# Routing tokens to experts with the 24 best of 16 groups, slots by counting, and matmuls on zeros

## The chip, the cores and the metric

The kernel runs on one core of a Trainium2 chip. The metric is the device time of one execution in microseconds (us). The engines of the core work side by side, each through its own queue in order: TensorE (PE in the profile; its weight loads are PEld), VectorE (DVE), ScalarE (ACT), GpSimd (POOL), and the DMA queues, most of them filled by SyncE (SP). SBUF is the working memory of 128 partitions; PSUM is the memory that TensorE writes.

## The reference

Attention over 8 batches, 8 heads, 576 positions and 64 dimensions, in which each query keeps its 32 best keys. The heads side by side give 4608 tokens of 512 features, and each token goes to one of 8 experts; each expert takes only its 80 tokens of highest gate weight.

```python
scores = scale * np.matmul(q, k.transpose(0, 1, 3, 2))
kth = np.partition(scores, -top_k, axis=-1)[..., -top_k:-top_k + 1]
scores = np.where(scores >= kth, scores, -1e9)
attn = softmax(scores); x = (attn @ v) as (4608, 512)
logits = x @ w_gate                         # (4608, 8)
expert_idx = np.argmax(logits, axis=1)
gate_w = probs[np.arange(N), expert_idx]    # softmax of the logits
for e in range(E):
    tok_idx = where(expert_idx == e)
    if len(tok_idx) > capacity:             # capacity is 80
        keep = np.argpartition(-gate_w[tok_idx], capacity)[:capacity]
        tok_idx = tok_idx[keep]
    h = np.maximum(x[tok_idx] @ w1[e], 0.0) # 512 -> 1024
    out[tok_idx] = gate_w[tok_idx, None] * (h @ w2[e])
```

All other rows of the output are zero.

## The kernel before, in words

**Attention** (`Attention.run`) goes over 32 pairs of heads, each in 5 blocks of queries (four of 128, one of 64 in which the two heads share the partitions). One block of 128 queries of one head is a unit; there are 288. The order of work of all engines is written out by hand, in `step`, as a pipeline over units: VectorE searches the threshold of a unit (`parts`, `search`), GpSimd makes the mask (`below`, L239), TensorE forms scores, turns them and multiplies with v, ScalarE copies and exponentiates. The end of each pair of heads writes its token features to HBM and adds to the logits (`norm`). Every second batch, after its last pair of heads, `gates` turns the logits of the two batches into gate weights: VectorE finds the maximum, a one-hot of the first best expert (`oh`, L359 to L362) and the gate weight (`gw`, L365 to L367). GpSimd multiplies the one-hot with the token number and with the gate weight and writes both to `R` (L376): 128 partitions, two kinds, 40 token columns, 8 experts. So `gates` runs four times, the last time when attention is done.

`judge` (L466 to L478) makes a flag, `bad`, from the smallest threshold and the smallest sum. It is read at the end of the kernel (L699): if set, a slow exact version of everything runs after.

**Routing** is the first half of `finish` (L511 to L603). One expert's 80 best among 4608 tokens are found in two stages. First, four transposes on TensorE (L534) put the gate weights of `R` on 80 partitions (10 groups by 8 experts), with 512 tokens each, and `best` (L526, L528) finds each partition's 80 best: MAX8 gives eight values, MATCH_REPLACE8 wipes them out, ten times. Then 10 matmuls with slices of the identity (L542) bring the 10 lists of each expert side by side, 800 values on 8 partitions, and `best` finds the 80 best of those. The 80th is the expert's bar. The bar goes to all partitions (L550 to L556); `sel` (L562) marks the tokens above or on it; matmuls with ones and a scan (L569 to L579) number the marked tokens, so that each has a slot from 1 to 80 (L581). `hot` (L588) is the one-hot of the slot, 80 wide, and 40 matmuls (L591) with it as weights gather token numbers and gate weights into `acc`, 80 slots by 16. A matmul of float32 operands is two instructions on TensorE. Four small operations (L594 to L603) make indices of it.

**Experts**: `gather` (L616) fetches the 80 rows of one expert by an indirect DMA, `turn_g` (L626) transposes them, `hidden` (L639) and `product` (L651) multiply, `store` (L660 to L663) transposes back, scales and writes by an indirect DMA. The order is again by hand (L667 to L686). Weights of experts 0 to 3 are loaded during attention; those of expert 4 when attention has ended, and those of experts 5 to 7 when the product of an earlier expert gives its buffer free.

Of the kernel before, what the change touches and what calls it, by code (L numbers as in the profile page):

```python
# [9 lines left out]
F32 = mybir.dt.float32  # L10
BF16 = mybir.dt.bfloat16
I32 = mybir.dt.int32
AX = mybir.AxisListType.X
Act = mybir.ActivationFunctionType
Alu = mybir.AluOpType
PSUM = bass.MemoryType.PSUM
# [4 lines left out]
FAR = 1e-30  # L21
# [4 lines left out]
def kernel(  # L26
# [11 lines left out]
    nc = tc.nc  # L38
# [17 lines left out]
    FK = F // P  # L56
    NG = 6
    G0 = 24
    UPP = 2 * NF + 1
    NU = NP * UPP  # L60

# [9 lines left out]
    nc.gpsimd.memset(zero, 0.0)  # L71
    wg = const.tile([P, HP, E], F32, name="wg")

    R = const.tile([P, 2, NM, E], F32, name="R")
    nc.gpsimd.memset(R, 0.0)
    bad = const.tile([1, 1], I32, name="bad")

# [41 lines left out]
    class Attention:  # L119
# [226 lines left out]
        def gates(self, b0, nb):  # L346

            GM = nb * NK
            lg = self.lg.rearrange("p b c e -> p (b c) e")
            small = lambda sh, name: self.small.tile(sh, F32, name=name, tag=name, bufs=1)  # L350
            mx = small([P, GM], "mx")
            nc.vector.tensor_reduce(mx, lg, axis=AX, op=Alu.max)
            nc.vector.tensor_tensor(out=lg, in0=lg, in1=mx.unsqueeze(2).to_broadcast([P, GM, E]), op=Alu.subtract)
            el = small([P, GM, E], "el")
            yield 0
            nc.scalar.activation(el, lg, Act.Exp)

            oh = small([P, GM, E], "oh")
            nc.vector.scalar_tensor_tensor(out=oh, in0=lg, scalar=0.0, in1=rank.unsqueeze(1).to_broadcast([P, GM, E]),  # L359
                                           op0=Alu.is_ge, op1=Alu.mult)  # L360
            nc.vector.tensor_reduce(mx, oh, axis=AX, op=Alu.max)
            nc.vector.tensor_tensor(out=oh, in0=oh, in1=mx.unsqueeze(2).to_broadcast([P, GM, E]), op=Alu.is_equal)  # L362
            yield 0
            gw = small([P, GM], "gw")
            nc.vector.tensor_reduce(gw, el, axis=AX, op=Alu.add)  # L365
            nc.vector.tensor_scalar(gw, gw, EPS, None, op0=Alu.add)
            nc.vector.reciprocal(gw, gw)  # L367
            yield 0
            ms = bass.ds(b0 * NK, GM)
            for p, cs in ((P, slice(0, NF)), (TL, slice(NF, NK))):  # L370
                sh = [p, nb, cs.stop - cs.start, E]
                o4 = oh.rearrange("p (b c) e -> p b c e", b=nb)[:p, :, cs, :]
                for kind, src in ((0, tok[:, ms]), (1, gw)):
                    r4 = R[:p, kind, ms, :].rearrange("p (b c) e -> p b c e", b=nb)[:, :, cs, :]
                    s4 = src.rearrange("p (b c) -> p b c", b=nb)[:p, :, cs].unsqueeze(3).to_broadcast(sh)
                    nc.gpsimd.tensor_tensor(out=r4, in0=o4, in1=s4, op=Alu.mult)  # L376

        def run(self, slow):

# [83 lines left out]
                    i += 1  # L463
            assert not slow and not due

        def judge(self):  # L466

            small = self.small
            least = small.tile([P, 2], F32, name="least", bufs=1)
            nc.vector.tensor_reduce(least[:, 0:1], thr_all, axis=AX, op=Alu.min)  # L470
            nc.vector.tensor_reduce(least[:, 1:2], z_all.rearrange("p n c h -> p (n c h)"), axis=AX, op=Alu.min)
            nc.vector.tensor_scalar(least[:, 1:2], least[:, 1:2], -FAR, None, op0=Alu.add)
            nc.vector.tensor_tensor(out=least[:, 0:1], in0=least[:, 0:1], in1=least[:, 1:2], op=Alu.min)
            ps = self.ps_c.tile([P, 512], F32, name="tp", tag="cc")
            nc.tensor.transpose(ps[:1, :P], least[:, 0:1], ident)
            low = small.tile([1, 1], F32, name="low", bufs=1)
            nc.vector.tensor_reduce(low, ps[:1, :P], axis=AX, op=Alu.min)
            nc.vector.tensor_scalar(bad, low, 0.0, None, op0=Alu.is_le)  # L478

        def batch(self, b):  # L480

            for hp in range(HP):
# [12 lines left out]
                for _ in self.norm(hp, b, hp, 0, 1):  # L495
                    pass

    def finish(wpool):

        stack = ctx.enter_context(ExitStack())  # L500
        late = stack.enter_context(tc.tile_pool(name="late", bufs=1))
        for dma in load_w(4, late):
            dma()
        sl = stack.enter_context(tc.tile_pool(name="sl", bufs=1))
        routing = stack.enter_context(ExitStack())
        ps_a = routing.enter_context(tc.tile_pool(name="ps_a", bufs=2, space=PSUM))
        ps_b = routing.enter_context(tc.tile_pool(name="ps_b", bufs=4, space=PSUM))

        rt = routing.enter_context(tc.tile_pool(name="rt", bufs=1))
        iot_i = rt.tile([P, cap], I32, name="iot_i")  # L510
        nc.gpsimd.iota(iot_i, pattern=[[1, cap]], base=1, channel_multiplier=0)  # L511
        iot = rt.tile([P, cap], F32, name="iot")
# [4 lines left out]
        before = rt.tile([P, P], BF16, name="before")  # L517
        nc.gpsimd.affine_select(out=before, in_=onesb, compare_op=Alu.is_gt, fill=0.0, base=0,
                                pattern=[[1, P]], channel_multiplier=-1)
        EH = E // 2  # L520
        seg = rt.tile([P, EH, 2 * NM], F32, name="seg")
        nc.gpsimd.memset(seg, 1.0)
        nc.gpsimd.memset(seg[:, :, 0:1], 0.0)
        def best(dst, src):
            for r in range(0, cap, 8):
                nc.vector.max(out=dst[:, r : r + 8], in_=src)  # L526
                if r + 8 < cap:
                    nc.vector.match_replace(out=src, in_to_replace=dst[:, r : r + 8], in_values=src, imm_value=0.0)  # L528


        NH = 10
        cd_ps = ps_b.tile([P, 512], F32, name="cd_ps", tag="b")
        for i in range(NM // NH):
            nc.tensor.transpose(cd_ps[: NH * E, i * P : (i + 1) * P], R[:, 1, i * NH : (i + 1) * NH, :].rearrange("p m e -> p (m e)"), ident)  # L534
        cd = rt.tile([NH * E, NM // NH * P], F32, name="cd")
        nc.vector.tensor_copy(cd, cd_ps[: NH * E, : NM // NH * P])
        top1 = rt.tile([NH * E, cap], F32, name="top1")
        best(top1, cd)
        mg_ps = ps_a.tile([P, 2, 512], F32, name="mg_ps", tag="a")
        GH = NH // 2  # L540
        for g in range(NH):
            nc.tensor.matmul(mg_ps[:E, g // GH, g % GH * cap : (g % GH + 1) * cap], lhsT=ident[: NH * E, g * E : (g + 1) * E],  # L542
# [7 lines left out]
        nc.vector.tensor_scalar_max(thr, top2[:, cap - 1 : cap], 1e-6)  # L550
        thrw = rt.tile([E, P], F32, name="thrw")
        nc.vector.tensor_copy(thrw, thr.to_broadcast([E, P]))
        tb_ps = ps_b.tile([P, 512], F32, name="tb_ps", tag="b")
        nc.tensor.transpose(tb_ps[:, :E], thrw, ident[:E, :E])
        tb = rt.tile([P, E], F32, name="tb")
        nc.vector.tensor_copy(tb, tb_ps[:, :E])  # L556
# [2 lines left out]
        sel = rt.tile([P, E, 2, NM], BF16, name="sel")  # L559
        tbb = tb.unsqueeze(2).to_broadcast([P, E, NM])  # L560
        for i, op in enumerate((Alu.is_gt, Alu.is_equal)):
            nc.vector.tensor_tensor(out=sel[:, :, i, :], in0=R[:, 1, :, :].rearrange("p m e -> p e m"), in1=tbb, op=op)  # L562
        w = rt.tile([P, E, 2, NM], F32, name="w_slot")
        tot = ps_a.tile([P, 2, 512], F32, name="tot", tag="a")
        pos = ps_a.tile([P, 2, 512], F32, name="pos", tag="a")
        C = EH * 2 * NM
        for i in range(2):
            sv = sel[:, i * EH : (i + 1) * EH, :, :].rearrange("p e k m -> p (e k m)")
# [12 lines left out]
        nc.vector.tensor_reduce(slot, w.rearrange("p e k m -> p m (e k)"), axis=AX, op=Alu.add)  # L581


        acc = ps_b.tile([P, 512], F32, name="acc", tag="b")
        CH = NM // 4
        for m0 in range(0, NM, CH):
            hot = rt.tile([P, CH, cap], F32, name="hot", tag="hot", bufs=2)
            nc.vector.tensor_tensor(out=hot, in0=slot[:, m0 : m0 + CH].unsqueeze(2).to_broadcast([P, CH, cap]),  # L588
                                    in1=iot.unsqueeze(1).to_broadcast([P, CH, cap]), op=Alu.is_equal)
            for m in range(m0, m0 + CH):  # L590
                nc.tensor.matmul(acc[:cap, : 2 * E].rearrange("p (k e) -> p k e", k=2), lhsT=hot[:, m - m0, :], rhs=R[:, :, m, :],  # L591
                                 start=(m == 0), stop=(m == NM - 1))
        a2 = sl.tile([cap, 2, E], F32, name="a2")
        nc.vector.tensor_copy(a2, acc[:cap, : 2 * E].rearrange("p (k e) -> p k e", k=2))  # L594
        i1 = a2[:, 0, :]
# [60 lines left out]
        def store(e):  # L656
            ps = ps_x.tile([P, 512], F32, name="yx", tag="x")
            yT = y_t.pop(e)
            for d in range(HP):
# [4 lines left out]
                out=out[:, :], out_offset=bass.IndirectOffsetOnAxis(ap=idx_s[:, e : e + 1], axis=0),  # L664
                in_=y[:, :], element_offset=0, bounds_check=N - 1, oob_is_err=False, in_offset=None)

        with tc.manual_schedule():  # L667
            for e in range(3):
                gather(e)
            turn_g(0)  # L670
            turn_g(1)
            for e in range(E + 1):
                if e < E:
                    hidden(e)
                if e >= 2:
                    store(e - 2)
                if e >= 1:
                    product(e - 1)
                    if 5 <= e + 4 < E:
                        for dma in load_w(e + 4, wpool):  # L680
                            dma()
                if e + 3 < E:
                    gather(e + 3)
                if e + 2 < E:
                    turn_g(e + 2)
            store(E - 1)  # L686
# [3 lines left out]
    with ExitStack() as main:  # L690
# [3 lines left out]
        with ExitStack() as stack:  # L694
            att = Attention(stack, False)
            att.run(slow)
            att.judge()
        finish(wpool)
    with tc.If(nc.values_load(bad[0:1, 0:1]) > 0):  # L699
        for dma in clear():  # L700
            dma()
# [4 lines left out]
        with ExitStack() as again:  # L706
            wpool = again.enter_context(tc.tile_pool(name="wpool2", bufs=4))
            for e in range(4):
                for dma in load_w(e, wpool):
                    dma()  # L710
            finish(wpool)


# [29 lines left out]
```

## Time and profile before

| | before |
|---|---|
| time, median of 3 | 1154.14 us (1153.25 to 1154.17) |
| span of the profiled execution | 1156.5 us |
| TensorE busy | 921.9 us (80%) |
| VectorE busy | 999.5 us (86%) |
| ScalarE busy | 714.0 us (62%) |
| GpSimd busy | 520.7 us (45%) |
| mean granted TensorE clock | 0.922 |

The page of the profile gives busy times of each engine over the span and then, as rows of 40 digits, in equal slices of it: a digit is the busy share in tenths. The row PEclk is the clock that TensorE was granted, in tenths of full speed. The timeline lists work in order of time, and behind it, in brackets, for what the engine waited. In the list of groups, one line has all instructions of one kind from one source line: their count, busy time and mean in ns, then the idle time just before them and what ended it. Windows give busy times of all engines in a chosen stretch.

### The profile page before, as it was taken

How to read it: one execution, taken by the hardware profiler on the slowest of the kernel's cores; microseconds unless marked ns; L12 is line 12 of the kernel's file. 1: busy time of each engine (PE TensorE's matmuls, PEld its weight loads, DVE VectorE, ACT ScalarE, POOL GpSimd, SP SyncE). 2: the span in 40 equal slices, each digit the busy share in tenths (PEclk: the TensorE clock that was granted, in tenths of full speed). 3: DMA queues.
4: the chain of work that ended last, by engine and by line, in shares of the span. 5: the costliest groups of instructions: out<-in, count | busy, mean ns of one | idle time of the engine just before them, and what ended most of it. 6: DMA issues, size and time to landing. Idle time of an engine off the chain costs nothing.

```text
span 1156.5 us, 35811 instructions
## 1 busy us (share of the span) xinstructions
PE 921.9 (80%) x13262; PEld 753.3 (65%) x13262; DVE 999.5 (86%) x5218; ACT 714.0 (62%) x1534; POOL 520.7 (45%) x344
## 2 busy tenths in 40 slices
PE   6988888888888888888888888888888887207897
PEld 3766766666666666676667676666666666207886
DVE  6999999999999999999899999998999998691011
ACT  4777776777677777767677777776777766100110
POOL 2555554555555545555455545545555455001101
PEclk9999998999999899988999989998999988656999
DMA  4144442323232332332132211111111100402830
GB/s 107 34 115 116 115 116 70 79 79 79 79 79 79 79 79 79 79 79 79 48 81 71 62 33 43 39 42 34 42 43 43 43 12 12 156 0 71 312 128 27
DMA packets 167895, 85.77 MB, mean 74 GB/s; under 512 B 117792, under 2 KB 154656, under 8 KB 167712
## 3 DMA queue, kind: packets, MB, share of 16 engines
q1 hardware_dynamic: 166688, 80.78, 25.4%
q0 software_dynamic: 1024, 2.62, 0.7%
q8 instruction: 106, 1.74, 0.6%
q14 instruction: 77, 0.63, 0.2%
HBM read 63.19 MB, written 20.19 MB: 72 GB/s over the span
## 4 chain that ended last, share of the span: by engine, by line
DVE 49%; PE 26%; issue 12%; ACT 9%; POOL 3%; DMA 0%; SPq 0%; DVEq 0%; POOLq 0%; ACTq 0%
DVE cand L204 17%; PE cc L294 7%; DVE y L226 7%; DVE w L228 6%; DVE cand L223 6%; ACT s L197 4%; DVE top L215 3%; PE yp L651 3%; PE sp L169 3%; ACT wT L280 3%; PE ab L271 3%; POOL mask L239 2%; DVE pick L231 2%; DVE w L215 2%; DVE top L526 1%
## 5 line engine op out<-in xcount | busy, mean ns | idle before, releaser
L239 POOL TENSOR_SCALAR mask<-s,thr_all 128x576 bf16<-128x576 f32 x288 | 496.3, 1723 | 477.7 <-DVE cand L223 453.7
L204 DVE MAX8 cand<-s 128x8 f32<-128x96 f32 x1728 | 395.2, 242 | 8.8 <-ACT s L197 8.8
L220 ACT ACTIVATE sign<-s,w 128x576 bf16<-128x576 f32 x288 | 226.2, 786 | 118.1 <-DVE w L215 114.1
L294 PEld LDWEIGHTS cc<-vb,wT 128*64 128x64 f32 x5760 | 217.5, 149 | 36.9 <-ACT wT L280 20.1
L294 PE MATMUL cc<-vb,wT 128*64 128x65 f32 x5760 | 239.4, 236 | 2.6 <-ACT wT L280 1.1
L226 DVE SCALAR_TENSOR_TENSOR y<-s,w 128x576 f32<-128x576 f32 x288 | 228.8, 794 | 0.2 <-issue 0.2
L228 DVE MAX8 w<-y 128x8 f32<-128x576 f32 x288 | 212.3, 737 | 0.0
L192 PE MATMUL sp<-kT,qT 64*128 64x288 f32 (+1 forms) x1280 | 203.6, 438 | 5.0 <-ACT kT L180 2.5
L271 PE MATMUL ab<-ident,s 128*128 128x128 f32 x1152 | 187.6, 294 | 1.2 <-ACT wT L280 1.2
L197 ACT ACTIVATE s<-sp 128x1152 f32<-128x1152 f32 (+1 forms) x160 | 166.8, 1042 | 16.4 <-PE sp L192 16.2
L271 PEld LDWEIGHTS ab<-ident,s 128*128 128x128 f32 x1152 | 136.5, 149 | 25.8 <-ACT wT L280 14.8
L280 ACT ACTIVATE wT<-ab 128x1024 f32<-128x1024 f32 (+1 forms) x160 | 150.6, 941 | 0.0
L276 PEld LDWEIGHTS <-mask 128*128 128x128 bf16 x1440 | 94.9, 99 | 70.4 <-POOL mask L239 68.1
L192 PEld LDWEIGHTS sp<-kT,qT 64*128 64x128 f32 (+1 forms) x1280 | 106.3, 180 | 43.2 <-ACT s L197 4.1
L278 ACT ACTIVATE wT<-cc 128x256 f32<-128x256 f32 (+1 forms) x160 | 58.8, 368 | 108.8 <-PE cc L276 108.8
L276 PE MATMUL cc<-minus,mask 128*128 128x128 bf16 x288 | 64.4, 223 | 59.2 <-POOL mask L239 59.1
L215 DVE MAX8 top<-cand 128x8 f32<-128x48 f32 x576 | 108.0, 187 | 0.1
L223 DVE MATCH_REPLACE8 cand<-top,cand 128x48 f32<-128x48 f32 x576 | 107.8, 187 | 0.0
L276 PE MATMUL ab<-minus,mask 128*128 128x128 bf16 x1152 | 103.2, 221 | 0.0
L315 ACT ACTIVATE xn<-cc,z_all 128x64 f32<-128x64 f32 (+1 forms) x320 | 82.9, 317 | 1.9 <-DVE z_all L306 1.8
L271 PE MATMUL cc<-ident,s 128*128 128x128 f32 x288 | 81.8, 284 | 0.0
L169 PE MATMUL sp<-ident,xn 128*128 128x128 f32 x128 | 26.4, 341 | 42.5 <-ACT s L197 42.5
(164 smaller groups left out, 861.4 us busy)
## 6 DMA issues: line engine op xcount, KB each, us to landing
w<-in_moe_w_dram SPq DMA_DIRECT2D x32, 512.0 KB, 4.0
w<-in_moe_w_dram SPq DMA_DIRECT2D x8, 2048.0 KB, 13.0
out_dram<-zero SPq DMA_DIRECT2D x9, 1024.0 KB, 5.8
qn<-in_q_dram SPq DMA_DIRECT2D x64, 128.0 KB, 3.8
kn<-in_k_dram SPq DMA_DIRECT2D x64, 128.0 KB, 2.9
vb<-in_v_dram SPq DMA_DIRECT2D x64, 128.0 KB, 2.6
xd<-xn SPq DMA_DIRECT2D x32, 256.0 KB, 2.3
qn<-in_q_dram SPq DMA_DIRECT2D x32, 32.0 KB, 3.4
```

Source lines behind the costliest of these rows:

```text
L192: nc.tensor.matmul(o, lhsT=qT[d, t * P : t * P + m], rhs=kT[d, j * HS : (j + 1) * HS], start=True, stop=True)
L197: nc.scalar.activation(s[:, : g * S].rearrange("p (j c) -> p j c", c=HS), ps[:, : 2 * g, :HS], Act.Copy, scale=TINY)
L204: nc.vector.max(out=cand[:, j, :], in_=s[:, j * S // NG : (j + 1) * S // NG])
L220: nc.scalar.activation(sign, s, Act.Sign, bias=w9[:, 7:8], scale=-1.0, accum_out=cnt)
L223: nc.vector.match_replace(out=cand, in_to_replace=dst, in_values=cand, imm_value=LOW)
L226: nc.vector.scalar_tensor_tensor(out=y, in0=s, scalar=w9[:, 7:8], in1=s, op0=Alu.is_lt, op1=Alu.mult)
L228: nc.vector.max(out=w9[:, 8:], in_=y)
L239: nc.gpsimd.tensor_scalar(self.mask[i], self.s[i], self.thr[:, i : i + 1], None, op0=Alu.is_lt)
L271: nc.tensor.matmul(dst[h][c], lhsT=sc[:, keys[c]], rhs=ident, start=c == 0 or (c == NF and h == 0), stop=False, is_transpose=True, skip_gr ...
L276: nc.tensor.matmul(dst[h][c], lhsT=mk[:, keys[c]], rhs=minus, start=False, stop=True, skip_group_check=True)
L280: nc.scalar.activation(wT[:, : g * NF, :], ab.rearrange("p h c r -> p (h c) r")[:, : g * NF, :], Act.Exp, scale=scale / TINY)
L294: nc.tensor.matmul(cc[r : r + TL, o], lhsT=wT[:, j * NF + c if c < NF else 2 * NF + j, r0 : r0 + TL], rhs=vb[:, c, h, :], start=(c == 0), ...
```

## The change

The routing is written anew, in `route`, and the old one stays as `route_all` for the slow exact version alone.

- **Groups.** `R` now holds gate weights only, in an order that lets two transposes and two small matmuls put them on all 128 partitions: 16 groups by 8 experts, with 288 tokens each. `gates` writes it with three products on VectorE instead of four on GpSimd.
- **24 of each group.** The first search finds only the 24 best of each of the 16 groups (3 MAX8 and 2 MATCH_REPLACE8), and `max_index` gives their positions, from which the token number follows. The second search is over 16 x 24 = 384 values.
- **Slots by counts.** Each group counts how many of its 24 reach the bar; a matmul with a triangle mask gives the number in the groups ahead of it. Since each group's list is in descending order, its r-th value has the slot "number ahead + r". One one-hot of the number ahead (`first`, 104 wide), shifted by r, serves all 24 ranks, so 24 matmuls replace 40.
- **The flag.** 24 are enough if no group gives all 24 to one expert; and the number of slots must be 80. Both go into `judge`, which sets the flag to the full version otherwise.
- **The check moved**: `judge` stands behind `hidden(2)` now, since it needs the counts.
- **Zero products**: `warm` issues bf16 matmuls of zeros, 256 columns each, whose result nobody reads: 72 after the lists have been brought together, and 36 after the slots. They are for the TensorE clock.

```diff
-    R = const.tile([P, 2, NM, E], F32, name="R")
+    R = const.tile([P, NK, B, E], F32, name="R")
+    chunks = ((slice(0, 2), slice(0, 3, 2)), (slice(2, 4), slice(1, 4, 2)), (slice(4, 5), slice(4, 5)))
...
-                    nc.gpsimd.tensor_tensor(out=r4, in0=o4, in1=s4, op=Alu.mult)
+                nc.vector.tensor_tensor(out=r4, in0=o4, in1=s4, op=Alu.mult)
...
+        def warm(n):
+            t = ps.tile([P, 2 * P], F32, name="warm", tag="warm", bufs=1)
+            z = zero.bitcast(BF16)
+            for _ in range(n):
+                nc.tensor.matmul(t, lhsT=z[:, :P], rhs=z, start=True, stop=True)
...
+            for r in range(0, TOP, 8):
+                src = cd_ps[:, :GS] if r == 0 else cd[:, r // 8 - 1, :]
+                nc.vector.max(out=top1[:, r : r + 8], in_=src)
+                if r + 8 < TOP:
+                    nc.vector.match_replace(out=cd[:, r // 8, :], in_to_replace=top1[:, r : r + 8], in_values=src, imm_value=0.0)
...
+            for g in range(GB):
+                nc.tensor.matmul(mg_ps[:E, g * TOP : (g + 1) * TOP], lhsT=ident[:, g * E : (g + 1) * E], rhs=top1,
+                                 start=True, stop=True)
+            warm(WARM1)
+            for r in range(0, TOP, 8):
+                nc.vector.max_index(out=ix[:, r : r + 8], in_max=top1[:, r : r + 8],
+                                    in_values=cd_ps[:, :GS] if r == 0 else cd[:, r // 8 - 1, :])
...
+            nc.tensor.matmul(few[:, 0:1], lhsT=ofe.rearrange("k g e -> k (g e)"), rhs=bar8, start=True, stop=True)
...
+            nc.vector.scalar_tensor_tensor(out=taken, in0=top1, scalar=bar, in1=ones, op0=Alu.is_ge, op1=Alu.mult,
+                                           accum_out=count[:, 0:1])
+            nc.tensor.matmul(few2[:, 0:1], lhsT=ahead, rhs=count[:, 0:1], start=True, stop=True)
+            nc.tensor.matmul(few2[:, 1:2], lhsT=same.rearrange("p g e -> p (g e)"), rhs=count[:, 0:1], start=True, stop=True)
...
+            nc.vector.tensor_scalar(first, col, few2[:, 0:1], None, op0=Alu.is_equal)
+            for r in range(TOP):
+                nc.tensor.matmul(acc[:cap, : 2 * E], lhsT=first[:, TOP - r : TOP - r + cap],
+                                 rhs=give[:, r, :, :].rearrange("p k e -> p (k e)"), start=(r == 0), stop=(r == TOP - 1))
+            warm(WARM2)
...
-            att.judge()
-        finish(wpool)
+        finish(wpool, False)
...
+                if e == 2 and not full:
+                    judge()
```

Further preparations of the new routing are a mask of the expert of each partition (`emask`), two masks made from it for the counts (`same`, `ahead`), the column numbers (`col`), and the first token of each group (`base_i`, `bi`, `base`).

## The prediction

> **What bounds the kernel now.** I read the page's slices first, for where the engines are full.
>
> ```profile
> span 1156.5 us, 35811 instructions
> PE   6988888888888888888888888888888887207897
> DVE  6999999999999999999899999998999998691011
> PEclk9999998999999899988999989998999988656999
> ```
>
> A slice is 28.9 us. For 34 slices VectorE (DVE) is at 9: attention is bound by it, and an operation added there costs nearly its full time. Then come two slices in which TensorE (PE) falls to 2 and 0 while its clock is at half: the routing. The timeline shows its edges.
>
> ```profile
> 991.10 0.22 DVE L367 RECIPROCAL gw<-gw 128x10 f32<-128x10 f32 x1
> ...
> 1007.66 2.83 PE L542 MATMUL mg_ps<-top,ident 80*8 80x80 f32 x20 [15.13 <-DVE top L526]
> ...
> 1032.40 1.36 DVE L562 TENSOR_TENSOR sel<-R,tb 128x320 bf16<-128x320 f32 x2
> ...
> 1041.49 10.85 PE L591 MATMUL acc<-R,hot 128*80 128x16 f32 x80 [6.45 <-DVE hot L588]
> ...
> 1058.98 3.94 PE L639 MATMUL hp__17147<-xt,w 128*64 128x80 f32 x64
> ```
>
> (Start and duration in us, then the work, and in brackets what it waited for.) Routing runs as one chain from the end of L367, 991.32, to the first expert matmul of L639, 1058.98: **67.7 us** in which nothing else is on the path. The groups of DVE in 988 to 1058 us say what fills it:
>
> ```profile
> L526 DVE MAX8 top<-mg 8x8 f32<-8x800 f32 x10 | 9.8, 982 | 0.3
> L528 DVE MATCH_REPLACE8 mg<-top,mg 8x800 f32<-8x800 f32 x9 | 8.7, 963 | 0.0
> L526 DVE MAX8 top<-cd 80x8 f32<-80x512 f32 x10 | 6.9, 691 | 0.3
> L528 DVE MATCH_REPLACE8 cd<-top,cd 80x512 f32<-80x512 f32 x9 | 6.0, 671 | 0.0
> ```
>
> Those searches are about 35 us with their loads and gaps. The other view I need is windows, for the clock:
>
> ```profile
> 990.00:995.00 5.00, 0.44 (x1) 0.14 (x1) 3.51 (x11) 0.00 (x0) 0.94 (x4) 0.55 0.94 376
> 1040.00:1052.00 12.00, 10.51 (x79) 10.52 (x80) 4.28 (x5) 0.00 (x0) 0.00 (x0) 0.50 0.00 1
> 1057.00:1062.00 5.00, 4.51 (x54) 4.13 (x56) 0.98 (x2) 0.00 (x0) 2.40 (x3) 0.50 0.43 126
> 1062.00:1067.00 5.00, 5.00 (x136) 4.82 (x134) 0.49 (x1) 0.88 (x2) 0.00 (x0) 0.99 0.14 28
> ```
>
> The columns are busy time of PE, its weight loads, DVE, ACT, POOL, then the granted clock. PE was busy for 10.5 us in L591 and still held at 0.50, so narrow matmuls (16 columns) do not lift the clock; the expert matmuls lift it about 5 us after they begin.
>
> [...] PE idles from 988.9, the clock falls near 990.5, and the edges seen at 970, 976.8, 990.5 and 1062.1 are whole multiples of 3.4 us apart. [...]
>
> **The change, part by part.** The length law first. MAX8 takes 0.98 us on 800 elements and 0.69 on 512, so 0.29 per 288. A MAX8/load/MATCH_REPLACE8 pair takes 2.10 us on 800 (starts 1011.53 to 1013.63) and 1.51 on 512 (993.29 to 994.80): 2.05 ns per element and 0.46 fixed. Partitions do not matter (8 and 80 lie on one line).
>
> *Gates.* Three DVE products replace four on GpSimd. L341, as small, takes 0.19 us in the full stream. Three earlier calls: 9 x 0.19 = **+1.7** (0.9 if they overlap as L598 and L601 do, starting 0.08 apart); I take 1.5. GpSimd loses its four at nothing: it is 45% busy and mostly waits for DVE. In the last call the products come after L367: 0.5. Five small preparations enter DVE's queue among the gates (emask, bi, three on base) where iot leaves it: +0.5 net, between 0.3 and 1.0. bi waits for GpSimd's base_i, the sixth operation from 988.8, at a spacing of 0.15 done by 989.8, before DVE gets there; behind bi would be the whole gate chain, so a late one shows at once.
>
> *Turning R:* two 128x128 transposes, four narrow instructions, at half clock: 0.44 (the last L534) + 0.25 + 0.2 = 0.9.
>
> *First search:* 3 MAX8 and 2 replacements on 288: two pairs of 1.05, one MAX8 of 0.46: **2.6**, where before it was 15.0 with the copy L536.
>
> *Positions:* three index passes. Lower bound, a replacement of the same length with its load, 0.53[...]. I take 0.58, so 1.75, plus three 24-element operations at 0.18: 2.3. They hide the 16 mg matmuls (32 instructions; L542 took 0.14 each at half clock and 80 columns, with 24 columns 0.05, 1.6 us). The old mg wait of 3.0 and copy of 1.0 vanish.
>
> *Second search:* 384 columns instead of 800: nine pairs of 1.25 and one MAX8 of 0.55: **11.7**, before 19.9.
>
> *First zero products (72).* They stand in PE's queue ahead of the bar's matmul few, for which DVE waits. 128x320 bf16 at half clock came every 0.27 (L569, L570), so 256 columns cost 0.21 at half and 0.107 at full. Begun when mg is through, [...] 24 run slow and 48 fast: 10.3 us. DVE needs 0.6 + 11.7 = 12.3 from the same start. So they cost nothing; the work that hides them is the second search. If all ran slow: 15.4, and few is 2.9 late.
>
> *Bar, counts, give.* Clamp, matmul, copy, count: L550 to L556 took 0.92 for such a round trip; with a two-pass matmul and an accumulator read (0.08 in L231's groups) 1.2. Two products, give on 384 (L577 on 320: 0.48, so 0.55), and first: 1.2, beside the two count matmuls.
>
> *Slots.* 24 matmuls in 48 instructions replace 80. L591's 10.85 us over 80 is 0.136 at half clock: **6.5**; at full clock half, 3.3. All of sel, scan, slot and hot goes.
>
> *Second zero products (36)* stand ahead of the gathered tokens' transposes. L591's end to L639 was 6.64 us, waiting for indices and two gathers. [...] the 36 end after some 6.0; two warm transposes and the copy make it 7.05. Then the first half of expert 0 runs warm: 2.2 instead of 3.9, **-1.65**.
>
> *Check moved* into expert 2: seven DVE operations, about 1.9 us, begin after the fourth xt copy while PE has 4.6 us of L639; one PE transpose stays, 0.15. Taking it out of the end of attention gains nothing: L478 ended at 987.9, and DVE then waited for ACT's part until 988.75.
>
> Sum from 991.3 to the first expert matmul: 0.5 + 0.5 + 0.9 + 2.6 + 2.3 + 11.7 + 1.2 + 1.2 + 6.5 + 7.05 = 34.45 instead of 67.7: -33.2. With +1.5, +0.15 and -1.65: **-33.2, 1121 us**. Expert 4's weights, issued at 988.66, move in the windows up to about 1001 and are not met by gathers at 1016 or later; the loads of experts 5 to 7 hang on the products before them and shift along.
>
> **Rivals.**
> *A, clock lost before the slots* (the sum above, 1121). For it: after the zero products PE idles about 3.5 to 5 us, and 988.9 to 992 shows how soon the clock drops; L591 shows that the slots don't raise it.
> *B, clock stays full.* Slots 3.3, no delay by the 36, transposes as the gathers land: 6.4. The stretch is 30.6: 67.7 - 30.6 + 1.65 - 1.65 = -37.1, **1117**. For it: the 72 may run slower than 0.107 each and end nearer to few; against it: the edges must fall well.
> *C, zero products in the way*: half clock throughout, few 2.9 late, the 36 take 7.7, expert 0 not warmed: 1121 + 2.9 + 2.0 + 1.65 = **1127.5**. For it: 970 to 976.8, where PE was full and the clock stayed at half[...]; against it: 1062.
> *D, slower than before.* If a group gave all 24 or a tie broke the count, the flag would run everything again: at least 288 searches of 4 MAX8 at 0.74, so over 1121 + 850 = **1970**. From the inputs of the reference the fullest group gives 16 and no bar ties: hardly.
>
> **How the numbers follow.** A 0.57, B 0.23, C 0.10, a smaller gain from something unseen (a late preparation, instruction fetch) 0.08, D 0.02. The time is A's. Index passes, preparations and gates are worth about 1.5 either way around A and B; the range 1115.5 to 1125 covers both and leaves out C and D. Faster by over 0.2% (2.3 us) 0.97, within 0.005, slower 0.025.
>
> **What would show it.** DVE's searches: pairs of 1.05 and 1.25 us. PE: no wait of DVE's bar on zero products; acc at 0.134 an instruction (A, C) or 0.067 (B); clock by windows of 3 us from the end of the 72; the first L639 group's 64 instructions in 2.2 us. The attention part longer by 1.5. It would be wrong if acc's start came more than 24 us after L367, if DVE waited for a preparation, or if expert matmuls waited for weights now needed 33 us sooner.

## The result

| | before | after |
|---|---|---|
| time, median of 4 | 1153.7 us (1152.95 to 1154.17) | 1118.24 us (1117.08 to 1120.55) |
| ratio to before | | 0.9696 (0.9679 to 0.9713) |
| span of the profiled execution | 1156.5 us | 1118.8 us |
| mean granted TensorE clock | 0.922 | 0.945 |

The change makes the kernel 35.5 us faster. The slices of the page after:

```profile
span 1118.8 us, 35976 instructions
PE   6888888888788888888888888888788888768997
DVE  5999999999999999999999999999899999962111
PEclk9999989999999989998899999999899989987999
```

The two slices in which TensorE stood at 2 and 0, under a clock of 6 and 5, have gone; what is left of them is a slice with TensorE at 6, and a clock of 8 and 7 in that slice and the next. The timeline of the routing, with start and duration in us, the work, and in brackets what it waited for:

```profile
990.98 0.22 DVE L371 RECIPROCAL gw<-gw 128x10 f32<-128x10 f32 x1
991.39 0.37 DVE L379 TENSOR_TENSOR R<-oh,gw 128x32 f32<-128x32 f32 x3
...
992.89 0.47 DVE L638 MAX8 top<-cd_ps 128x8 f32<-128x288 f32 x1 [1.13 <-PE cd_ps L631]
...
995.44 0.46 DVE L648 FIND_INDEX8 ix<-top,cd_ps 128x8 uint32<-128x288 f32 x1
...
996.90 8.92 PE L623 MATMUL warm<-zero 128*128 128x256 bf16 x72
...
997.44 0.55 DVE L660 MAX8 top<-mg_ps 8x8 f32<-8x384 f32 x1
...
1009.05 0.14 DVE L665 TENSOR_SCALAR bar<-top 8x1 f32<-8x1 f32 x1
...
1009.34 0.55 PE L667 MATMUL few<-bar,ofe 8*128 8x1 f32 x2 [3.52 <-DVE bar L665]
...
1011.96 6.59 PE L692 MATMUL acc<-give,first 128*80 128x16 f32 x48 [0.44 <-DVE first L687]
1018.38 6.16 PE L623 MATMUL warm<-zero 128*128 128x256 bf16 x36
...
1025.47 2.13 PE L754 MATMUL hp__17220<-xt,w 128*64 128x80 f32 x52 [0.37 <-DVE xt L743]
```

From the end of L371 (991.20) to L754 (1025.47) it is 34.3 us, instead of 67.7. The 72 zero products end at 1005.8, and TensorE then waits 3.5 us for the bar: they are in nobody's way. The windows of the same execution show the clock (the first number after the busy times and counts of the five engines):

```profile
999.00:1005.00 6.00, 6.00 (x57) 5.38 (x55) 5.65 (x16) 0.00 (x0) 0.00 (x0) 1.00 0.31 119
1006.00:1009.00 3.00, 0.00 (x0) 0.00 (x0) 2.84 (x7) 0.00 (x0) 0.00 (x0) 1.00 0.00 0
1009.00:1012.00 3.00, 1.58 (x7) 1.47 (x7) 1.75 (x10) 0.00 (x0) 0.00 (x0) 0.50 0.00 0
1012.00:1018.00 6.00, 6.00 (x46) 6.00 (x46) 0.00 (x0) 0.00 (x0) 0.00 (x0) 0.50 0.00 0
```

It is full from 998.8, 1.9 us after the 72 begin, until 3 us after their end, and half from 1009 on, just before the work that could have used it: the slots run 6 us at full occupancy and half clock.

### The profile page after: what moved, and what is told of

Read it like the earlier page. It is cut to its first block, busy times and chain, and to the rows that moved or that the text cites. A ratio compares the mean times of both kernels' runs of the same rounds, so it can differ in the third digit from the quotient of the medians.

```text
span 1118.8 us, 35976 instructions
## 1 busy us (share of the span) xinstructions
PE 926.0 (83%) x13353; PEld 755.2 (68%) x13353; DVE 972.1 (87%) x5213; ACT 714.0 (64%) x1534; POOL 515.7 (46%) x332
## 3 DMA queue, kind: packets, MB, share of 16 engines
q8 instruction: 107, 1.75, 0.6%
## 4 chain that ended last, share of the span: by engine, by line
DVE 47%; PE 28%; issue 11%; ACT 10%; POOL 2%; DMA 1%; SPq 0%; DVEq 0%; POOLq 0%; ACTq 0%
DVE cand L208 17%; DVE y L230 7%; PE cc L298 7%; DVE w L232 6%; DVE cand L227 6%; ACT s L201 5%; DVE top L219 4%; PE sp L173 3%; PE yp L766 3%; PE ab L275 3%; ACT wT L284 3%; DVE pick L235 2%; POOL mask L243 2%; DVE w L219 2%; PE sp L196 1%
## 6 DMA issues: line engine op xcount, KB each, us to landing
w<-in_moe_w_dram SPq DMA_DIRECT2D x8, 2048.0 KB, 12.9
```

## The experiments

In the diffs a minus is the changed kernel. "Stretch" is the routing from the last gate reciprocal to the first expert matmul; "attention" ends with that reciprocal; the "tail" goes from the end of expert 0's first 64 instructions to the end of the span. These three come from one profiled execution each, the times and ratios from several executions each, the ratios against executions of the kernel before on the same chip ("160 first" and "before, again" are single executions).

| kernel | time, us | ratio to before | attention | stretch | expert 0, first 64 | tail |
|---|---|---|---|---|---|---|
| before | 1153.7 | | 991.3 | 67.7 | 3.9 | 93.6 |
| before, again | 1154.5 | | 988.2 | 67.7 | 3.8 | 93.0 |
| after | 1118.2 | 0.9696 (0.9679 to 0.9713) | 991.2 | 34.3 | 3.0 | 90.3 |
| after, again | 1118.0 | 0.9691 (0.9677 to 0.9705) | 991.1 | 34.3 | 2.4 | 90.4 |
| no zero products | 1122.8 | 0.9731 (0.9712 to 0.9750) | 993.8 | 34.0 | 4.5 | 92.8 |
| the 36 alone | 1121.6 | 0.9728 (0.9709 to 0.9747) | 987.9 | 34.9 | 2.4 | 93.6 |
| 104 first | 1117.5 | 0.9689 (0.9663 to 0.9716) | 989.7 | 32.3 | 2.4 | 92.3 |
| 160 first | 1124.2 | | 988.4 | 38.0 | 2.4 | 93.7 |
| gates on GpSimd | 1117.5 | 0.9684 (0.9658 to 0.9709) | 987.0 | 34.6 | 2.4 | 91.7 |
| gates eight times | 1132.7 | 0.9835 (0.9813 to 0.9856) | 1001.1 | 34.3 | 2.4 | 89.9 |
| 32 best of a group | 1127.0 | 0.9776 (0.9754 to 0.9798) | 989.2 | 40.8 | 2.4 | 91.6 |
| strips | 1112.7 | 0.9647 (0.9631 to 0.9664) | 989.5 | 29.6 | 2.4 | 91.5 |
| strips, 104 first | 1113.5 | 0.9657 (0.9644 to 0.9671) | 987.6 | 28.9 | 2.4 | 92.8 |
| strips, gates on GpSimd | 1112.8 | 0.9640 (0.9609 to 0.9671) | 989.7 | 29.5 | 2.4 | 91.0 |

**No zero products at all, and the 36 alone.**

```diff
-    WARM1, WARM2 = 72, 36
+    WARM1, WARM2 = 0, 0        # the second kernel: 0, 36
```

> Both groups of zero products are left out (72 and 36). Reference marks of the changed kernel: slots (acc) 6.59 us, from their end to the first expert matmul 6.92, first 64 instructions of expert 0 some 2.8. Account of the prediction (A): the 72 lie beside the second search and the clock has dropped before the slots anyway, so slots stay at 6.5 to 6.6 and the bar's matmul starts as soon as VectorE is done; without the 36 the first expert matmul comes 6.6 us after the slots instead of 6.9, but the first half of expert 0 runs at half clock, 3.9 us. Net 0.6 to 1.3 us slower than the changed kernel: about 1119.2. Rival 1, zero products do hold the clock for something in the routing: 2 us or more slower, 1120.5 or above. Rival 2, they stand in the way: faster than the changed kernel by 0.5 or more.

> The 72 zero products are left out, the 36 stay. Account A: nothing changes, slots 6.5 to 6.6 us at half clock, expert 0 warm, within 0.5 us of the changed kernel (1118.2). Rival, the 72 do something for the bar's and count matmuls (0.55 us each now): slower by 0.5 to 1.

Within the routing the first account held: slots 6.58 us in both, and the stretch 34.0 and 34.9 us. The time of the kernel without any did not fit it: 1122.8 us, where 1119.2 was expected. That lies where rival 1 put it, but not for rival 1's reason, since nothing in the routing got longer. Without the 36 the first expert matmul came 6.7 us after the slots, and the first half of expert 0 took 4.5 us instead of 2.4. This is the timeline of TensorE without zero products:

```profile
1025.85 0.77 PE L741 MATMUL xp<-ident,xg 80*128 80x80 f32 x4 [4.76 <-DMA xg<-xd,idx_x]
1027.04 0.80 PE L741 MATMUL xp<-ident,xg 80*128 80x80 f32 x4 [0.41 <-DMA xg<-xd,idx_x]
1027.76 4.51 PE L754 MATMUL hp__17112<-xt,w 128*64 128x80 f32 x64
```

So the 36 trade 0.3 to 0.9 us of delay for 2.1 us in expert 0: worth 1.2 to 1.8 us, an estimate from these profiles. The ratios of the two kernels, 0.9731 and 0.9728, have intervals of 0.002 to either side, too wide to show it. With the 36 alone:

```profile
1008.66 6.58 PE L692 MATMUL acc<-give,first 128*80 128x16 f32 x48 [0.44 <-DVE first L687]
1015.08 6.77 PE L623 MATMUL warm<-zero 128*128 128x256 bf16 x36
...
1022.78 2.44 PE L754 MATMUL hp__17148<-xt,w 128*64 128x80 f32 x64 [0.37 <-DVE xt L743]
```

The slots take the same 6.58 us. Its expected time, within 0.5 us of the changed kernel, missed: it is 3.3 us slower by the medians. In the profile the stretch is 0.6 us longer (the 36 took 6.77 us instead of 6.16) and the tail 3.2; that the two profiled executions are nonetheless equally long, 1118.8 us, is due to an attention 3.3 us shorter in this one, within its spread. More on the tail below.

**104 and 160 zero products in the first group.**

```diff
-    WARM1, WARM2 = 72, 36
+    WARM1, WARM2 = 104, 36     # the second kernel: 160, 36
```

> 104 zero products in the first group instead of 72, so that they end about 1009.3, as VectorE comes to the bar (in the changed kernel they ended at 1005.8, 3.2 us ahead, and the clock dropped at 1009.0). Account A [...] the slots begin 2.7 us after the bar's matmul, so they run between 3.3 us (full) and 6.6 (half), depending on where the edges fall: some 1.5 us faster than the changed kernel on average, 1116.5, if the zero products end in time. Rival 1: slots stay at 6.6, nothing changes (1118.2). Rival 2: the zero products end after VectorE, the bar's matmul waits for them by 0.5 to 2 us and the time is 1119 to 1120.

> 160 zero products in the first group instead of 72: with 24 of them at half clock they last about 20 us, 8 us beyond where the 72 ended. Account A: TensorE's queue is in order, so the bar's matmul starts some 4 to 6 us after VectorE has the bar (0.26 us after in the changed kernel), and the slots then run at full clock, 3.3 to 4.5 us; the stretch is 35 to 38 us. Rival: zero products don't hold up the bar's matmul, stretch 31 to 32.5.

With 104, windows:

```profile
1009.00:1010.00 1.00, 0.56 (x7) 0.47 (x6) 0.82 (x3) 0.00 (x0) 0.00 (x0) 1.00 0.00 0
1010.00:1011.00 1.00, 1.00 (x16) 1.00 (x16) 0.00 (x0) 0.00 (x0) 0.00 (x0) 0.96 0.00 0
1011.00:1012.00 1.00, 1.00 (x10) 1.00 (x9) 0.00 (x0) 0.00 (x0) 0.00 (x0) 0.50 0.00 0
```

The slots (from 1009.80) begin at full clock, 16 instructions in a microsecond, and fall back to 10 when the clock drops at 1010.9, with TensorE at full occupancy. They took 5.66 us: the full clock reached 1.1 us into them, and the slots did not bring it back. The 1.5 us expected on average were the author's estimate; the stretch came out 2.0 us shorter, yet the time did not fall measurably (0.9689, against 0.9696 and 0.9691): in this profile the tail is 1.9 us longer. With 160, the timeline of TensorE:

```profile
1012.56 0.38 PE L667 MATMUL few<-bar,ofe 8*128 8x1 f32 x2
...
1014.59 4.99 PE L692 MATMUL acc<-give,first 128*80 128x16 f32 x48 [0.45 <-DVE first L687]
```

and that of VectorE in the same execution:

```profile
1006.23 0.14 DVE L665 TENSOR_SCALAR bar<-top 8x1 f32<-8x1 f32 x1
1012.98 0.16 DVE L669 COPY bar<-few 128x1 f32<-128x1 f32 x1 [6.60 <-PE few L667]
```

VectorE has the bar at 1006.4 and TensorE takes it up at 1012.56: 6.2 us in the queue behind zeros, against 1.6 us gained on the slots. The stretch of 38.0 us is the upper end of what was expected; the delay is just above its range (4 to 6), and the slots, at 4.99 us, are outside theirs (3.3 to 4.5), because the clock dropped 1.9 us into them. This is the cost that rival C feared, made visible; with 72 it does not arise. The 160 lasted 18.55 us, where some 20 was the author's estimate.

**The gates' products, moved back and multiplied.**

```diff
-                nc.vector.tensor_tensor(out=r4, in0=o4, in1=s4, op=Alu.mult)
+                nc.gpsimd.tensor_tensor(out=r4, in0=o4, in1=s4, op=Alu.mult)
```

> The three products of the gates go back to GpSimd, with the new R. As predicted, they cost VectorE 0.19 us each in a full stream: the nine of the three earlier calls gone make attention 1.5 to 1.7 us shorter, the last call becomes 0.3 us longer: 1.2 us faster than the changed kernel, 1117.0; the last reciprocal of the gates ends 1.5 us sooner than 991.20. Rival: attention is not set by VectorE's instruction count alone (in the changed kernel it did not get longer although nine products were added: 991.20 against 991.32), so that reciprocal stays within 0.5 us and the time is the changed kernel's plus 0.3, 1118.5.

```diff
+                for _ in range(8 if isinstance(b0, int) and b0 < B - 2 else 1):
+                    nc.vector.tensor_tensor(out=r4, in0=o4, in1=s4, op=Alu.mult)
```

> In the three earlier calls of the gates each of the three products on VectorE is written eight times, 63 more operations of 0.16 to 0.19 us. As predicted, each costs its time in full, 0.1 (overlapping) to 0.19 us: attention 6 to 12 us longer, time 1124 to 1130. Rival, attention has slack on VectorE (its length went from 987 to 994 us among kernels with the same attention code), so that most of it is absorbed: less than 3 us longer, time under 1121.

Moving them back settles nothing: the reciprocal ended at 987.0, but with them on VectorE it has ended anywhere from 987.6 to 993.8, and the ratio of 0.9684 lies within the interval of the changed kernel's. Multiplied, they stand clear of that spread. One call in the timeline of VectorE:

```profile
300.85 4.93 DVE L380 TENSOR_TENSOR R<-oh,gw 128x32 f32<-128x32 f32 x24
```

24 products in 4.93 us, 0.205 each, and attention ended at 1001.1, 7 to 13.5 us later than in those, for 63 x 0.205 = 12.9 us of added work. VectorE hides none of it that could be seen, and the rival fell. The time, 1132.7 us, is above the 1124 to 1130 expected: it is 14.4 us over the changed kernel's by the medians, more than the 12.9, and the one profile does not show where the rest lies. So nine products in the changed kernel cost about 1.85 us by their durations, and 2.1 by the added time (14.4 / 63 x 9); both are estimates.

**32 of each group.**

```diff
-    TOP = 24
+    TOP = 32
```

> The 32 best of each group instead of 24 (16 x 32 = 512 values in the second search). Account A: the whole routing is one chain on VectorE and then the slots at half clock, so each added length counts in full: first search one more pair 1.06 us, one index pass 0.43, second search 19 passes and loads of 128 more columns 2.5, give 0.15, slots 16 more instructions at 0.137, 2.2: 6.4 us. The stretch from the last gate reciprocal to the first expert matmul is 40.7 us instead of 34.3, the time about 1124.5. Rival: part of it lies beside other work (the lists' matmuls, the zero products), and the stretch grows by less than 5 us.

The stretch was 40.8 us, against 40.7 expected: slots 8.71 us for 64 instructions, and each pass longer by its columns. The routing is one chain, and the lengths of its passes add. The time, 1127.0 us, is 2.5 us over what was expected; 1.2 us of that stand in the tail of this profile.

**The slots in strips.**

```diff
-            for r in range(TOP):
-                nc.tensor.matmul(acc[:cap, : 2 * E], lhsT=first[:, TOP - r : TOP - r + cap], rhs=give[:, r, ...], ...)
+            for r in range(TOP):
+                u = r % 4 * 32
+                nc.tensor.matmul(st_ps[u : u + 32, :cap], lhsT=giv[:, r, :], rhs=first[:, TOP - r : TOP - r + cap],
+                                 start=(r < 4), stop=(r >= TOP - 4))
+            nc.vector.tensor_copy(strips, st_ps[:, :cap])
+            nc.tensor.matmul(acc[:cap, : 2 * E], lhsT=strips, rhs=summer, start=True, stop=True)
```

(giv is give with 16 columns of zeros behind it; summer adds the four strips.)

> The slots' matmuls turned round: the 32-column give (16 of them zeros) is the weight, the shifted one-hot of 80 columns streams, and four ranks run side by side in four column strips of TensorE; a copy and one matmul with a summing matrix add the strips. Account A, the slots are bound by loading 80 columns of float32 weights at half clock, 0.137 us an instruction: four strips side by side take 0.036 to 0.07 each, 1.7 to 3.4 us in all, plus copy 0.25 and matmul 0.5 with its waits: from the first strip to the end of acc 2.6 to 4.2 instead of 6.6, the stretch 30.3 to 31.9 us, time 2.4 to 4 us below the changed kernel. Rival, the bound is the streaming or the issue of an instruction and strips don't run side by side in float32 (48 x 0.14): stretch 35 or more.

```profile
1010.06 1.82 PE L698 MATMUL st_ps<-first,giv 128*32 128x80 f32 x48 [0.37 <-DVE first L691]
1011.96 0.24 DVE L701 COPY strips<-st_ps 128x80 f32<-128x80 f32 x1 [1.89 <-PE st_ps L698]
1012.26 0.45 PE L702 MATMUL acc<-summer,strips 128*80 128x16 f32 x2 [0.37 <-DVE strips L701]
```

48 instructions take 1.82 us, 0.038 each instead of 0.137, and with copy and sum it is 2.65 us instead of 6.6. The stretch is 29.6 us, a little under the range expected, and the time 1112.7: this version beats both kernels (0.9647 against 0.9696 and 0.9691, with intervals apart). The edit changes two things together, the number of weight columns and the strips; which of them gave how much was not separated.

> The strips together with 104 zero products in the first group. Account A: the clock is full at the start of the slots in most executions (the slots begin 2.7 us after the bar's matmul and now last under 3 us), so they take 1.3 to 2.6 us with copy and matmul and the stretch is 29 to 30.5 us: about 1 us better than the strips with 72. Rival: without gain over the strips with 72 zero products, as the clock has dropped (stretch within 0.4 us), or worse if the bar's matmul waits.

With 104 zero products the strips took 1.73 us with copy and sum, at full clock, and the stretch was 28.9, 0.7 us better, but the tail was 1.2 us longer and the time no better: 0.9657 against 0.9647, intervals overlapping.

> The strips (72 zero products) together with the gates' products on GpSimd. The kernel with each product eight times showed 0.205 us of VectorE for each (24 in 4.93 us), so nine of them are 1.85 us of attention: expected 1.85 - 0.3 = 1.5 us below the strips alone, 1111.2, stretch 29.8 us. Rival: no difference, since executions of the same attention differ by more (1112.7).

No difference from the strips alone could be measured, 0.9640 (0.9609 to 0.9671) against 0.9647. The 1.5 us are smaller than the interval.

**Both kernels once more.**

> The kernel before, once more. If the attention part and the waits of TensorE for instructions differ by execution and not by kernel, its last gate reciprocal ends anywhere between 986 and 994 us and the part from the end of expert 0's first half to the end is 90 to 94 us with 2.4 to 5.4 us of waits put down to issue; the stretch of the routing stays at 67.7 within 0.7. Rival: the 93.6 us and 5.3 us of the first look belong to this kernel and come again within 0.3.

> The changed kernel once more, against the kernel before. Account A: the 72 zero products bring nothing and the 36 about 1 us, so the 0.9728 and 0.9731 of the kernels without them, against 0.9696 at first, are partly the spread of executions: expected ratio 0.971 to 0.972. Rival, the 72 are worth 3 us somewhere: the ratio comes again at 0.9696 within 0.001. In either case the stretch of the routing is 34.3 us within 0.6, and the attention part ends anywhere between 987 and 994 us.

The stretches came again within 0.1 us, 67.7 and 34.3. The kernel before ended its attention 3.1 us sooner than at first. The ratio after came again at 0.9691, so the 3 to 4 us that separate it from the kernels without the 72 zero products are not the spread of one comparison, and account A of this run was wrong.

**The tail.** The waits of TensorE in the tail, kernel before:

```profile
PE yp L651 <- issue: 3.5, 6, 1.1
...
PE hp__17734 L639 <- issue: 1.1, 1, 1.1
PE hp__17573 L639 <- issue: 0.7, 1, 0.7
```

and the kernel after, from its first expert matmul on:

```profile
PE yp L766 <- issue: 1.8, 6, 0.3
...
PE hp__17659 L754 <- issue: 0.4, 1, 0.4
...
PE hp__17220 L754 <- issue: 0.2, 1, 0.2
```

The columns are total, times and longest. "Issue" is time in which TensorE waited for nothing that the profile shows: 5.3 us before, 2.4 after (0.2 of it among expert 0's first 64 instructions), in the same expert code. Over all profiles, the seven with 72 zero products have tails of 89.9 to 91.7 us (mean 90.9), the seven others (before twice; none; the 36 alone; 104 twice; 160) 92.3 to 93.7 (mean 93.1). The clock is not what parts them: in 13 of the 14 it was full from the start of the tail to TensorE's last instruction; with the gates on GpSimd it was half for 3.4 us, and its 91.7 are the longest of the seven.

The waits themselves have a pattern in the traces. The page lists a DMA queue that carries instructions:

```profile
q8 instruction: 107, 1.75, 0.6%
```

107 packets and 1.75 MB are 16 KB a packet. In the 14 tails TensorE has 69 waits put down to issue, 58.5 us together. The 55 of them that last 0.38 us or more make 54.2 us, and every one of the 55 ends 1.2 to 1.5 us after a 16 KB packet of instructions has landed. Counted from the start of TensorE's stream in the trace, weight loads and control instructions included, they stand at the same few places in all kernels: the instructions 23234, 23490, 23746, 24002, 24258, 24514, 24770 and 25026, 256 apart, each within one. A packet lands about every 5 us there, so chance would not do this. So TensorE, in these waits, was very likely waiting for its next 16 KB of instructions. This is a coincidence in time and place, without an experiment on it. The zero products shift the code of the experts against these places; why that makes some of the waits vanish with 72 of them, and not with fewer or more, stays open.

## Why the prediction held

The forecast was 1121 us by the clock being lost before the slots (A), with 1115.5 to 1125; measured 1118.24. Its steps, one by one, in the profile after:

- *Routing*: the 34.45 expected include 0.5 of preparations ahead of the reciprocal, so 33.95 stand against the 34.3 measured behind it. Products of the last call 0.56 (0.5), transposes 1.13 (0.9), first search 2.49 (2.6), positions 2.06 (2.3), second search 11.6 (11.7), bar to count 1.36 (1.2), products to slots 1.55 (1.2), slots 6.59 (6.5), to the expert 6.92 (7.05). The law of 2.05 ns per element and 0.46 us per pair carried both searches; pairs came every 1.06 and 1.23 us. That partitions do not matter could not follow from the two lengths it was read from, since any two points lie on one line; here it does: MAX8 took 0.47 us for 288 elements on 128 partitions and 0.55 for 384 on 8, where the slope between 512 and 800 elements gives 0.46 and 0.56. One small slip in the sum: nine pairs of 1.25 and 0.55 make 11.8, not 11.7. That the 36 zero products end after some 6.0 us was the author's estimate; they took 6.16.
- *Preparations*, +0.5: from the last addition to the logits (L345) to the end of the reciprocal it is 2.74 us, against 2.57 before, so about 0.2. VectorE did wait 0.22 us for one of them, which the prediction had named as a sign of being wrong; it is too short to matter:

```profile
989.71 0.38 DVE L589 TENSOR_REDUCE emask<-ident 128x8 f32<-128x128 f32 x1 [0.22 <-POOL base_i L611]
```

- *Positions*: an index pass came every 0.43 us, where the author's estimate was 0.58. FIND_INDEX8 took 0.46 us, as its replacing sister on the same length (0.45), and even the lower bound of 0.53 us a pass was too high.
- *Clock.* A, not B: half clock in the slots. The 72 took 8.9 us, not 10.3, because the clock rose 1.9 us after they began; that 24 of them run slow (at 0.21 us each, 5.0 us) was the author's estimate. TensorE was busy for 3.23 of the 3.41 us before that rise, as the matmuls that bring the lists together end just ahead of the zeros. The wait of TensorE for the bar, 3.5 us, shows the step right that they cost nothing. The clock rose at 998.8, dropped at 1009.0 and rose at 1022.6, after 10.24 us at full and 13.65 at half; in the clock records of the two traces every value is 0.5 or 1, and every stretch between two changes lasts a whole multiple of 3.41 us, from one to 27 of them. It dropped also when TensorE had not been idle throughout: in the 3.41 us before the drops at 970.0 and 990.5 in the kernel before, the profile has TensorE busy for 1.10 and 1.48 us. And the expert matmuls of L639 lifted it 3.2 us after they began (1058.98 to 1062.14), not 5 as the prediction reads it. B could be had only in part: with 104 and 160 zero products the slots still took 5.66 and 4.99 us, as the clock dropped within them and did not come back until they had ended.
- *Gates*, +1.5: about 1.85 to 2.1, estimated from the kernel that has them eight times. In a single pair of profiles it is invisible: attention ended at 991.3 and 988.2 before and 991.2 and 991.1 after, and the spread from one execution to the next is larger than the cost.
- *Expert 0*, -1.65: from 3.9 to 2.4 in ten profiles with a warm clock; in the first profile after it was 3.0, with waits put down to issue among its instructions (0.24 us of the matmuls, 0.40 of their weight loads).
- *The check* in expert 2 costs 0.11 us of TensorE, as expected, and the first part of its VectorE work ends 3 us before TensorE takes it up:

```profile
1042.19 0.16 DVE L792 TENSOR_REDUCE one<-least 128x1 f32<-128x4 f32 x1
...
1045.07 0.27 PE L794 MATMUL jp<-ident,one 128*1 128x128 f32 x1
...
1045.18 0.60 PE L775 MATMUL yx<-ident,yT 128*80 128x128 f32 x4
```

What the sum lacked is the tail, 2.9 us shorter (93.3 to 90.4 as means of two profiles each): the prediction took it as unchanged, and that term accounts for the 2.8 us between forecast and measurement. It had given instruction fetch a small chance of making the gain smaller; the waits that look like it made the gain larger, and no step foresaw that. The routing's own saving, 33.4 us, is the step that decided, and it was right for the reasons given. With the gates (an estimate of 1.85) and expert 0 (1.1 as means of two profiles), the measured parts add to 33.4 + 2.9 + 1.1 - 1.85 = 35.6 us, against 35.5. So the 3 to 4 us that the kernel with 72 zero products has over those without them come mostly from the tail, not from the clock for which they were put in. Of the rivals, C's delay was produced at 160 and is absent at 72, and no run shows D.

## What to carry to other kernels

In a stretch that is one chain, price each pass from two lengths of the same operation in the trace (a slope and a fixed part, here 2.05 ns an element and 0.46 us a pair) and add them up. Ask of each filler in whose queue it stands (160 zero products held the bar's matmul back for 6.2 us, 72 did not), and look also at the code behind it: the tails with 72 zero products were 2.2 us shorter on average than the others. In the slots the weight loads took as long as the matmuls (6.48 of 6.59 us). Turning the operands round, so that fewer columns are loaded, and putting four accumulations side by side in column strips gave 4.0 us there, where 32 more zero products gave 2.0 in the stretch and nothing in the time. And mark off the part that the change touches: whole-kernel times here spread by up to 0.9% among executions, while the stretch of one kernel repeated within 0.1 us.

## What the runs showed of the hardware

- Full occupancy of TensorE did not always raise the clock: the slots (float32, 80 weight columns, 16 streamed) ran 6 us busy at 0.50, and when the clock was full at their start it dropped 1.1 us in (104 zero products) and 1.9 us in (160) and stayed at half to their end.
- A float32 matmul with 32 weight columns and 80 streamed, four column strips in turn, took 0.038 us an instruction at half clock, against 0.137 with 80 weight columns, 16 streamed and no strips.
- FIND_INDEX8 took 0.46 us on 288 elements, as long as MATCH_REPLACE8 (0.45); with its load it came every 0.43 us.
- Attention, the same code, ended between 987.6 and 993.8 us in the kernels that have its gates on VectorE as the change has them, with nothing in the routing to set it.
- In the experts TensorE stood still for 2.3 to 5.8 us in all, put down to issue; all the waits of 0.38 us or more ended 1.2 to 1.5 us after a 16 KB packet of instructions had landed, at places 256 instructions apart. Why their sum depends on the number of zero products issued ahead is open.
